# Four side-by-side products in the local attention output, and other transfer prices in the planner

## The chip, the cores and the metric

The kernel runs on one core of one Trainium2 chip, as one program. The metric is the device time of an execution in microseconds. A core has five engines that run side by side, each on its own list of instructions in fixed order: TensorE (PE), which multiplies matrices and writes the results into eight banks of PSUM; VectorE (DVE), ScalarE (ACT) and GpSimd (POOL), which work on elements; and SyncE (SP), which here issues nearly all transfers. The transfers run on DMA engines and land in SBUF or in device memory.

## The reference

Attention for 4 batches of 8 heads, 576 tokens of 64 features, is the sum of two parts; two expert layers follow on all 2304 tokens (512 features, 2048 hidden).

```python
q_d, k_d, v_d = (x.reshape(B, H, S // 4, 4, D).mean(axis=3) for x in (q, k, v))
out_up = np.repeat(sm_attn(q_d, k_d, v_d), 4, axis=2)          # pooled attention
mask = np.abs(pos[:, None] - pos[None, :]) < 4                 # local attention
scores = np.where(mask, scale * (q @ k.T), -1e9)
attn = exp(scores - max) ; attn = attn / (sum + 1e-9)
x = out_up + attn @ v                                          # per head
x = x.transpose(0, 2, 1, 3).reshape(B * S, H * D)
h = x @ w_in  ; x = (h * sigmoid(h)) @ w_out                   # layer 1
h = x @ w_in2 ; y = elu(h) @ w_out2                            # layer 2
```

## The kernel before

**Stages.** Attention works on 16 pairs of heads (four a batch). Layer 1's first half of the hidden features is computed beside it, in units of one block of 256 tokens and 128 hidden features: `first` (L983) multiplies the split input by the split weights, `second` (L1031) multiplies the activated result by the second weights. When these units are done, passes over pairs of token blocks follow (`paired`; first products on L1333, second ones on L1421 and L1423), for the rest of layer 1 and for layer 2. Numbers are carried as a high and a low part, so each product is three.

**One pair of heads** (`attend`). q and k rows are loaded (`load_rows`, L554), v for the pooled part (`load_v`, L558) and rows of v in ten overlapping windows of 64 (`load_windows`, L564 and L568). PE transposes q and k (L601), makes the local scores (`scores`, L712), the pooled scores (L765), and later transposes both softmax results (L818, L839). `out_d` (L857) gives the pooled output. `out_l` (L884) gives the local output, in two jobs of one half of the tokens (288) each: five windows by two heads, ten products with 64 rows and some 57 columns. Head j reads partitions 64j to 64j+63 and writes the same partitions of one PSUM bank, so the ten products alternate between two quarters of TensorE's array. `join` (L894, DVE) adds pooled and local output and writes x (`x32`). A product in 32-bit floats shows as two records in the trace.

The local scores use all four quarters: the windows alternate between column halves, the heads between row halves.

**The order of the work** is written out by a planner when the program is built. Each piece of work is a `Job` with an engine, an assumed duration, predecessors, buffers that it takes (`Hold`) and a due time. `pick` takes the job that can start first by the planner's clocks, among equals the one due first, and emits its instructions; each engine then runs its list in that order, whatever the real times are. For transfers the planner keeps one clock, `clock_of["dma"]`: a transfer begins after it, moves it on by the job's `dma` price, and lands a fixed time later; none is issued more than `BACKLOG` = 3 us ahead of it. Before the change the prices are 1.44 us for the rows of q or k of a pair, 1.6 for the window rows, 1.1 for v, 1.75 for a weight block of 512 KB, and 3.6 for the store of a batch's x.

```python
if self.dma is not None:
    clock_of["dma"] = max(clock_of["dma"], t + DMA_WAIT) + self.dma
    self.end = clock_of["dma"] + DMA_LAND
```

While `filling` is on (until layer 1's first unit is emitted) gaps that the planner sees on PE are filled with products of zeros (L328). `split_x` (L931 on ACT, L935 on GpSimd) splits x, `prepare` (L383 to L398, then L960 and L964) decodes and splits the weights. `keep_x` (L1070) stores a batch's x for the later passes; its job waits for all joins of that batch.

Of the kernel before, what the change touches and what calls it, by code (L numbers as in the profile page):

```python
# [15 lines left out]
ALU = mybir.AluOpType  # L16
# [6 lines left out]
def attention_moe_moe2_kernel(ctx, tc, q, k, v, wi1, wo1, wi2, wo2, out):  # L23
    nc = tc.nc
    B, H, S, D = q.shape
    NT, DM = out.shape
    DFF = wi1.shape[1]
    P = 128
    FAC = 4
    SD = S // FAC  # L30
    HS = SD // 2
# [10 lines left out]
    FP = NF // NPASS  # L42
# [131 lines left out]

    class Job:

        def __init__(self, eng, dur, fn, preds=(), gate=None, due=1e9, port=False, lat=0.1, other=None, takes=(), uses=(), dma=None, mode=None):
# [12 lines left out]
            self.sooner(due)  # L190
# [45 lines left out]
        def emit(self):  # L236
            t = self.start()
            assert t is not None
            cand.remove(self)
            for h in self.takes:  # L240
                h.take()
            if self.eng == "P":
                if filling[0]:
                    fill(t)
                mode_of[0] = self.mode
                now[0] = t + self.dur
            self.fn()
            clock_of[self.eng] = t + self.dur
            if self.port:
                clock_of["port"] = t + self.dur  # L250
            self.end = t + self.dur + self.lat
            if self.dma is not None:
                clock_of["dma"] = max(clock_of["dma"], t + DMA_WAIT) + self.dma
                self.end = clock_of["dma"] + DMA_LAND
# [110 lines left out]
    def decode_jobs(i, out, preds, takes=(), temp=None):  # L365
# [8 lines left out]
        if i < 2 * FP:  # L374
            held = [Hold(WS)]
            wst[i] = held[0]
            landed[i] = Job("S", 0.55, lambda: load_w(i), [], takes=held, dma=1.75)
        else:
            landed[i] = Job("S", 0.55, lambda: load_w(i), [decoded[i - WS_N]] if i >= 2 * FP + WS_N else [decoded[n] for n in range(2 * FP)], dma=1.75)

        def first():
            st = pairs_of(wst[i])
# [80 lines left out]
    def pool_matrix():  # L463
# [10 lines left out]
                )  # L474
        nc.vector.tensor_copy(m[WIN:P], m[:WIN])

    def pool_rows(w):

        return min(w0[1], w0[w + 1] - w0[w]) if w < NW - 1 else WIN
# [49 lines left out]
    def attend(i, due):  # L529
# [2 lines left out]
        h0 = 2 * pr  # L532
        early = b == 0
        packed = b < PACKED
        by_pe = b < PE_POOLED
# [35 lines left out]
        lq = Job("S", 1.1, lambda: load_rows(hq, q, nc.sync), [], takes=[hq], dma=cost)  # L571
        if early and pr < 2:
            lk = Job("A", 1.2, lambda: load_rows(hk, k, nc.scalar), [], takes=[hk], dma=cost)
        else:
            lk = Job("S", 1.1, lambda: load_rows(hk, k, nc.sync), [], takes=[hk], dma=cost)
        lw = Job("S", 2.2, load_windows, [], takes=[hw], dma=1.6)


        def tT():
# [2 lines left out]
        def row(which, c):  # L582
            return (hq, hk)[which].tile[:, c * 2 * D:(c + 1) * 2 * D]
# [6 lines left out]
        for n_, cells in enumerate(([(0, c) for c in range(NTB - 1)], [(1, c) for c in range(NTB - 1)], [(0, NTB - 1), (1, NTB - 1)])):  # L590
            bank = Hold(banks, "a")

            def flip(cells=cells, bank=bank):
                for n, (which, c) in enumerate(cells):
                    if packed:
                        for j in range(2):
                            nc.tensor.transpose(
                                bank.tile[j * D:(j + 1) * D, n * TB:(n + 1) * TB], row_of(which, j, c)[:TB], ident[:TB, :TB]
                            )
                    else:  # L600
                        nc.tensor.transpose(bank.tile[:, n * TB:(n + 1) * TB], row(which, c)[:TB], ident[:TB, :TB])  # L601

            used = {0: [hq], 1: [hk], 2: [hq, hk]}[n_]
            pj = Job(
                "P", (0.1 if packed else 0.085) * len(cells), flip, [lq] if n_ == 0 else [lk] if n_ == 1 else [lq, lk], lat=0.2,
                takes=[bank] + ([hqk] if n_ == 0 else []), uses=used, mode="t",
            )
            pj.after(prior)
            prior = [pj]
# [28 lines left out]
                    o += n  # L638


        red = Job(
            "V", 1.35, lambda: nc.vector.reduce_sum(hqkD.tile, hqk.tile.rearrange("p (m r) -> p m r", r=FAC), axis=AX.X),
            copies, takes=[hqkD], uses=[hqk],
        )
# [55 lines left out]
        for part, (s0, s1, halves_, outs) in enumerate(parts):  # L700
# [173 lines left out]
            for t in outs:  # L874
                bank = Hold(banks, "a")

                def out_l(t=t, bank=bank):
                    vw = hw.tile.rearrange("p (n d) -> p n d", d=D)
                    for w in range(t * NW // 2, (t + 1) * NW // 2):
# [11 lines left out]
                def join(t=t, bank=bank):  # L891
                    g0 = b * S + t * HALF
                    u0 = t * HALF // FAC
                    nc.vector.tensor_tensor(  # L894
                        x32[:, pr, g0:g0 + HALF].rearrange("p (m r) -> p m r", r=FAC),
                        bank.tile[:, :HALF].rearrange("p (m r) -> p m r", r=FAC),
                        haD.tile[:, u0:u0 + HALF // FAC].rearrange("p (m o) -> p m o", o=1).to_broadcast([P, HALF // FAC, FAC]),
                        op=ALU.add,
                    )

                pj = Job("P", 0.54, out_l, [lw] + [flips[g] for g in sorted(flips) if t == 1 or g == 0], lat=0.2, takes=[bank], uses=[hw, haT], mode="s")
                end_ = due[t] if isinstance(due, tuple) else due + 0.5 * t
                final.append(Job("V", 0.47, join, [pj, ups] + (sum(first_users.values(), []) if b == 1 else second_users if b else []), due=end_, uses=[bank, haD]))
                x_written[pr, 2 * b + t] = final[-1]
                if early:
                    first_users[pr].append(final[-1])
        batch_end.setdefault(b, []).extend(final)
        return final

# [535 lines left out]
    with tc.manual_schedule():  # L1445
# [52 lines left out]
            landed[i].due = W_AT  # L1498
        filler(WARM)
        constants()  # L1500
        pool_matrix()
        hpool.take()

        run(g1_jobs[0, 0])
        filling[0] = False
        run([j for b_ in range(B) for j in batch_end[b_]] + [kept_x[b_] for b_ in range(B)] + [x for p_ in w_split.values() for x in p_])
        PREFER.clear()
# [71 lines left out]
```

## Time and profile before

| | us |
|---|---|
| median of three runs | 909.17 |
| lowest | 908.99 |
| profiled execution | 908.4 |
| its span, first to last instruction | 906.7 |
| PE busy in the span | 886.6 |
| DVE busy | 640.9 |
| ACT busy | 535.1 |
| GpSimd busy | 258.7 |

One of the three runs took 2409.44 us; the median is not moved by it. The span is shorter than the execution by what lies around the first and last instruction. Attention ends at about 253 us of the span, layer 1's units at about 347 us. A row of the order of time reads: start, duration, engine, line, operation, what it writes and reads, shapes, the number of instructions merged, and in brackets the engine's idle time before it and what ended it.

### The profile page before, as it was taken

The numbers are of one execution on the slowest core, as the hardware profiler recorded it, in microseconds if no ns is written. First come the engines' busy times: TensorE is split into PE (matmuls) and PEld (weight loads), VectorE is DVE, ScalarE is ACT, GpSimd is POOL, SyncE is SP. The second block draws the span as 40 slices with busy tenths as digits, with TensorE's granted clock in tenths as the row PEclk, the third lists the DMA queues.
The fourth block names the chain that finished last, engine by engine and source line by source line (L and its number), as shares of the span: only waits on it lengthen the run. The fifth ranks groups of instructions, "written<-read, shape, count | busy, mean of one in ns | idle before, by whom it ended". The sixth has DMA issues, their size and how long they took to land.

```text
span 906.7 us, 17602 instructions
## 1 busy us (share of the span) xinstructions
PE 886.6 (98%) x6828; PEld 829.5 (91%) x6828; DVE 640.9 (71%) x1174; ACT 535.1 (59%) x1214; POOL 258.7 (29%) x280
## 2 busy tenths in 40 slices
PE   8979999999999999999999999999999999999998
PEld 5768899999999999999999999899898898998986
DVE  6888874556449847968948988669669889383562
ACT  4776474565447647637448568378388585471650
POOL 4687487666400101400105213001032023010000
PEclk9989899999999999999999999999999999999999
DMA  9796535353075121446153051340430530220301
GB/s 156 194 214 162 148 85 151 89 152 93 1 239 168 43 82 59 164 140 203 41 187 105 36 165 57 105 157 18 155 101 1 198 128 35 87 88 36 105 1 69
DMA packets 105730, 100.09 MB, mean 110 GB/s; under 512 B 62320, under 2 KB 88944, under 8 KB 105648
## 3 DMA queue, kind: packets, MB, share of 16 engines
q1 hardware_dynamic: 103280, 98.39, 36.8%
q8 instruction: 53, 0.87, 0.4%
q10 hardware_dynamic: 2368, 0.59, 0.4%
q14 instruction: 29, 0.24, 0.1%
HBM read 75.37 MB, written 23.59 MB: 109 GB/s over the span
## 4 chain that ended last, share of the span: by engine, by line
PE 57%; DVE 1%; issue 0%
PE b L1333 26%; PE b L1423 21%; PE b L1421 10%; DVE raw L398 0%; DVE part L1386 0%; DVE wl L1127 0%; DVE hgx L1231 0%; DVE raw L394 0%; DVE hg L1231 0%; DVE raw L391 0%
## 5 line engine op out<-in xcount | busy, mean ns | idle before, releaser
L1031 PE MATMUL b<-gh,wh 128*128 128x256 f32 x288 | 84.9, 295 | 0.0
L1031 PE MATMUL b<-gh,wl 128*128 128x256 f32 x288 | 82.4, 286 | 0.0
L1031 PE MATMUL b<-gl,wh 128*128 128x256 f32 x288 | 82.3, 286 | 0.0
L983 PE MATMUL b<-xh,wh 128*128 128x256 f32 x288 | 76.4, 294 | 0.2 <-DVE x L635 0.2
L1423 PE MATMUL b<-wl,grw 128*128 128x512 f32 x192 | 74.8, 389 | 0.0
L1423 PE MATMUL b<-wh,glk 128*128 128x512 f32 x192 | 74.8, 389 | 0.0
L1423 PE MATMUL b<-wh,ghk 128*128 128x512 f32 x192 | 74.7, 389 | 0.0
L1423 PE MATMUL b<-wh,grw 128*128 128x512 f32 x192 | 74.7, 389 | 0.0
L1333 PE MATMUL b<-xhr,wSA 128*128 128x384 f32 x288 | 74.5, 334 | 0.0
L983 PE MATMUL b<-xl,wh 128*128 128x256 f32 x288 | 73.8, 285 | 0.0
L983 PEld LDWEIGHTS b<-xh,wh 128*128 128x128 f32 x288 | 55.7, 193 | 2.1 <-issue 1.4
L1031 PEld LDWEIGHTS b<-gh,wh 128*128 128x128 f32 x288 | 55.9, 194 | 1.8 <-issue 1.2
L1031 PEld LDWEIGHTS b<-gl,wh 128*128 128x128 f32 x288 | 56.1, 195 | 0.0
L1031 PEld LDWEIGHTS b<-gh,wl 128*128 128x128 f32 x288 | 56.1, 195 | 0.0
L983 PEld LDWEIGHTS b<-xl,wh 128*128 128x128 f32 x288 | 55.7, 193 | 0.2
L1127 DVE TENSOR_TENSOR xlr<-xraw,xhr 128x768 fp32r<-128x768 f32 x46 | 44.4, 970 | 15.0 <-ACT xhr L1124 15.0
L1011 ACT ACTIVATE t<-b 128x256 f32<-128x256 f32 x72 | 27.5, 383 | 43.6 <-PE b L983 41.1
L1386 DVE SCALAR_TENSOR_TENSOR part<-b,part 128x384 f32<-128x384 f32 (+1 forms) x42 | 24.6, 612 | 40.1 <-PE b L1423 27.1
L1345 ACT COPY hg<-b 128x384 f32<-128x384 f32 x54 | 25.9, 480 | 45.7 <-PE b L1333 45.1
L1333 PEld LDWEIGHTS b<-xhr,wSA 128*128 128x128 f32 x288 | 52.1, 188 | 0.0
L983 PE MATMUL b<-xh,wl 128*128 128x256 f32 x288 | 50.7, 285 | 0.0
L1012 DVE SCALAR_TENSOR_TENSOR t<-t,b 128x256 f32<-128x256 f32 x72 | 29.9, 416 | 29.4 <-ACT t L1011 29.3
(289 smaller groups left out, 2803.4 us busy)
## 6 DMA issues: line engine op xcount, KB each, us to landing
ws<-in_moe_w_in_dram SPq DMA_DIRECT2D x32, 512.0 KB
ws<-in_moe_w_out_dram SPq DMA_DIRECT2D x32, 512.0 KB
xraw<-x SPq DMA_DIRECT2D x24, 384.0 KB
xd<-x SPq DMA_DIRECT2D x4, 1152.0 KB
yp<-yo SPq DMA_DIRECT2D x9, 512.0 KB
x<-part SPq DMA_DIRECT2D x6, 768.0 KB
yp<-yo SPq DMA_DIRECT2D x6, 768.0 KB
part<-yp SPq DMA_DIRECT2D x6, 768.0 KB
```

The costliest lines, as they stand in the source:

```text
L983: nc.tensor.matmul(ph.tile[:, :NB0], w[a][:, c, :], x_slot(n, c, b_), start=start and m == 0, stop=stop and m == len(products) - 1,)
L1011: th = Job("A", ACT_[NB0], lambda: nc.scalar.activation(tt(), h(), AF.Tanh, scale=0.5), [p2], takes=[t], uses=[ph])
L1012: st = Job("V", VEC_[NB0] + 0.02, lambda: nc.vector.scalar_tensor_tensor(tt(), tt(), 1.0, h(), op0=ALU.add, op1=ALU.mult), [th], uses=[ph])
L1031: nc.tensor.matmul(y[d // 2].tile[:, o:o + NB0], w[m // 2][:, sl], gg(m % 2), start=f == 0 and m == 0 and d % 2 == 0, stop=fin and m == 2, ...
L1127: other=("V", VEC_[width], lambda: nc.vector.tensor_tensor(lo(), src, hi().bitcast(F32), ALU.subtract)),
L1333: nc.tensor.matmul(acc_, a[:, cs], b[:, c, :], start=fresh and c == 0 and m == 0, stop=c == 1 and m == 2, skip_group_check=True,)
L1345: snap[after, j] = [Job("A", ACT_[NB], lambda dst=dst, acc_=acc_: nc.scalar.copy(dst, acc_), [], gate, due=soon)]
L1386: nc.vector.scalar_tensor_tensor(dst, src, sc, dst, op0=ALU.mult, op1=ALU.add)
L1421: nc.tensor.matmul(y[d][:, :NB], wm[:, sl], gm, start=first, stop=last_)
L1423: nc.tensor.matmul(y[d], gm[:, sl], wm, start=first, stop=last_)
```

## The change

For batches 2 and 3 (`QUAD_FROM = 2`) the two `out_l` jobs of a pair become one. It takes two banks, one for each half of the tokens, and walks through both halves in turn; in half 1 the heads write swapped column halves. So four successive products go to four different quarters. The adds of half 1 read swapped partitions and become two of 64 partitions each. Half 0 keeps its single add.

The planner's prices for transfers rise: rows of q and k to 1.6, window rows to 1.9, v to 1.5, weight blocks to 2.2 us. The store of batch 0's x waits for batch 1's joins instead of batch 0's (`X_AFTER = 1`). The other new names are set so that they change nothing (`POOL_QK = 0`, `FILL_TO = (0, 0)`, the `SAFE` values 0).

```diff
+    D_ROWS, D_LOCAL, D_V, D_W, S_ROWS, S_LOCAL, X_AFTER = 1.6, 1.9, 1.5, 2.2, 1.1, 2.2, 1
+    POOL_QK = 0
+    QUAD_FROM = 2
+    FILL_TO, SAFE_R, SAFE_W = (0, 0), 0.0, 0.0
-            landed[i] = Job("S", 0.55, lambda: load_w(i), [], takes=held, dma=1.75)
+            landed[i] = Job("S", 0.55, lambda: load_w(i), [], takes=held, dma=D_W, safe=SAFE_W)
-        cost = 1.05 if packed else 1.44
+        cost = 1.05 if packed else D_ROWS
-        lw = Job("S", 2.2, load_windows, [], takes=[hw], dma=1.6)
+        lw = Job("S", S_LOCAL, load_windows, [], takes=[hw], dma=D_LOCAL)
-            lv = Job("S", 1.1, load_v, [], takes=[hv], dma=1.1)
+            lv = Job("S", S_ROWS, load_v, [], takes=[hv], dma=D_V)
...
+            banko = [Hold(banks, "a") for _ in range(2)]
+
+            def out_l(banko=banko):
+                vw = hw.tile.rearrange("p (n d) -> p n d", d=D)
+                for i_ in range(NW // 2):
+                    for t in range(2):
+                        w = i_ + t * NW // 2
                         n = a0[w + 1] - a0[w]
                         c0 = (w % 2) * WIN + a0[w] - q0[w]
                         o = a0[w] - t * HALF
                         for j in range(2):
+                            p_ = (j + t) % 2 * D
                             nc.tensor.matmul(
-                                bank.tile[j * D:(j + 1) * D, o:o + n],
+                                banko[t].tile[p_:p_ + D, o:o + n],
...
+            pj = follow(Job("P", 0.75, out_l, [lw] + [flips[g] for g in sorted(flips)], lat=0.2, takes=banko, uses=[hw, haT], mode="s"), "pso")
+            for t, p0, p1 in ((0, 0, P), (1, 0, D), (1, D, P)):
...
+                    i0 = (p0 + t * D) % P
                     nc.vector.tensor_tensor(
-                        x32[:, pr, g0:g0 + HALF].rearrange("p (m r) -> p m r", r=FAC),
-                        bank.tile[:, :HALF].rearrange("p (m r) -> p m r", r=FAC),
+                        x32[p0:p1, pr, g0:g0 + HALF].rearrange("p (m r) -> p m r", r=FAC),
+                        bank.tile[i0:i0 + p1 - p0, :HALF].rearrange("p (m r) -> p m r", r=FAC),
...
-        kept_x[b] = Job("S", 0.6, go, batch_end[b], due=due, dma=3.6)
+        kept_x[b] = Job("S", 0.6, go, batch_end[max(b, X_AFTER)], due=due, dma=3.6)
```

## Rows read from the trace of the kernel before

**Rows 1.** The page, part 1: busy time, share, instructions of each engine.

```profile
PE 886.6 (98%) x6828; PEld 829.5 (91%) x6828; DVE 640.9 (71%) x1174; ACT 535.1 (59%) x1214; POOL 258.7 (29%) x280
```

**Rows 2.** Windows: length, busy PE, PEld, DVE, ACT, POOL; clock, DMA, GB/s.

```profile
120.00:253.00 133.00, 132.62 (x1715) 125.83 (x1714) 72.12 (x158) 71.95 (x228) 85.55 (x107) 1.00 0.35 94
253.00:347.00 94.00, 94.00 (x773) 94.00 (x772) 62.13 (x134) 54.06 (x122) 5.47 (x6) 1.00 0.40 128
...
386.00:906.00 520.00, 516.42 (x2710) 482.14 (x2710) 373.88 (x639) 306.29 (x603) 79.44 (x64) 1.00 0.29 97
```

**Rows 3.** Windows before 120 us; the last three are half-clock stretches.

```profile
54.00:62.00 8.00, 2.70 (x19) 2.35 (x19) 6.87 (x15) 5.32 (x15) 6.99 (x9) 0.81 1.21 237
...
84.00:90.00 6.00, 4.88 (x57) 4.06 (x58) 4.58 (x8) 3.31 (x8) 4.07 (x6) 0.69 0.02 4
...
59.02:65.84 6.82, 5.34 (x29) 5.34 (x30) 6.67 (x13) 4.34 (x13) 5.90 (x8) 0.50 1.14 231
...
86.33:93.15 6.82, 6.82 (x65) 5.99 (x64) 4.78 (x9) 3.58 (x9) 3.12 (x4) 0.50 0.12 27
...
106.81:110.21 3.40, 3.40 (x20) 3.06 (x20) 3.02 (x5) 0.63 (x3) 0.73 (x1) 0.50 0.05 11
```

**Rows 4.** Order of time of PE: its waits, and what ended them.

```profile
56.95 0.60 PE L601 MATMUL b<-ident,spare 96*128 96x96 f32 x5 [2.73 <-DMA spare<-in_q_dram]
...
60.50 1.03 PE L601 MATMUL b<-ident,nat 96*128 96x96 f32 x5 [2.57 <-DMA nat<-in_k_dram]
...
85.12 0.49 PE L839 MATMUL b<-ident,ring 72*72 72x72 f32 x4 [1.30 <-DVE ring L723]
...
106.22 0.52 PE L818 MATMUL b<-ident,ring 128*128 128x128 f32 x3 [1.75 <-DVE qk L630]
...
385.95 0.44 PE L1421 MATMUL b<-grw,wl 128*128 128x384 f32 x1 [1.33 <-DVE wl L1127]
```

**Rows 5.** Order of time of PE: local output L884, scores L712, successors.

```profile
230.42 0.79 PE L884 MATMUL b<-ring,vw 64*64 64x60 f32 x20
231.14 0.49 PE L839 MATMUL b<-ident,ring 72*72 72x72 f32 x4
...
249.77 1.38 PE L884 MATMUL b<-ring,vw 64*64 64x60 f32 x40
251.08 0.71 PE L857 MATMUL b<-ring,vd 72*64 72x144 f32 x8
...
73.18 0.81 PE L712 MATMUL b<-x 64*64 64x64 f32 x40
73.93 0.39 PE L983 MATMUL b<-xh,wh 128*128 128x256 f32 x1
```

**Rows 6.** Windows of one line: L884 in 141 to 251 us, L712.

```profile
sum 110.00, PE 11.51 PEld 10.18; mean PE 5.75 PEld 5.09
...
141.00:251.00 110.00, 5.85 (x280) 4.89 (x280) 1.00 0.34 89
```

**Rows 7.** Order of time of SP's queue: loads, and the stores of x.

```profile
49.42 0.91 SPq L554 DMA_DIRECT2D spare<-in_q_dram  x2
...
52.47 2.65 SPq L554 DMA_DIRECT2D nat<-in_k_dram  x2
...
72.25 0.58 SPq L1070 DMA_DIRECT2D xd<-x  x1
...
90.33 0.65 SPq L564 DMA_DIRECT2D vw<-in_v_dram  x1
...
136.45 0.56 SPq L1070 DMA_DIRECT2D xd<-x  x1
```

**Rows 8.** Order of time of POOL: splits done before the load waits end.

```profile
55.36 0.73 POOL L935 TENSOR_TENSOR xl<-x,xh 128x256 fp32r<-128x256 f32 x1
...
56.62 2.51 POOL L964 TENSOR_TENSOR wl<-wf,wh 128x512 fp32r<-128x512 f32 x2 [0.53 <-ACT wh L960]
```

**Rows 9.** Line L894, the add into x: ns min/median/max, first, last.

```profile
L894 DVE TENSOR_TENSOR x<-b,ring x28: 423/456/459, 26.2 to 252.6; 128x288 f32<-128x288 f32 x28
```

More of the change, by code (lines that the diff above doesn't have):

```diff
@@ L175, in attention_moe_moe2_kernel, with __init__ @@
     class Job:
-        def __init__(self, eng, dur, fn, preds=(), gate=None, due=1e9, port=False, lat=0.1, other=None, takes=(), uses=(), dma=None, mode=None):
+        def __init__(self, eng, dur, fn, preds=(), gate=None, due=1e9, port=False, lat=0.1, other=None, takes=(), uses=(), dma=None, mode=None, safe=0.0):
+            self.safe = safe
             self.eng, self.dur, self.fn, self.gate = eng, dur, fn, gate
@@ L253, in emit @@
                 clock_of["dma"] = max(clock_of["dma"], t + DMA_WAIT) + self.dma
-                self.end = clock_of["dma"] + DMA_LAND
+                self.end = clock_of["dma"] + DMA_LAND + self.safe
             for h in self.uses:
@@ L376, in decode_jobs @@
             wst[i] = held[0]
-            landed[i] = Job("S", 0.55, lambda: load_w(i), [], takes=held, dma=1.75)
+            landed[i] = Job("S", 0.55, lambda: load_w(i), [], takes=held, dma=D_W, safe=SAFE_W)
         else:
-            landed[i] = Job("S", 0.55, lambda: load_w(i), [decoded[i - WS_N]] if i >= 2 * FP + WS_N else [decoded[n] for n in range(2 * FP)], dma=1.75)
+            landed[i] = Job("S", 0.55, lambda: load_w(i), [decoded[i - WS_N]] if i >= 2 * FP + WS_N else [decoded[n] for n in range(2 * FP)], dma=D_W, safe=SAFE_W)
         def first():
@@ L475, in pool_matrix, with poolers, pool_matrices @@
         nc.vector.tensor_copy(m[WIN:P], m[:WIN])
+    def poolers():
+        n = len(POOLED_BY) * HS
+        return natv[:, n:n + 2 * (TB // FAC)].rearrange("p (n m) -> p n m", n=2)
+    def pool_matrices():
+        m = poolers()
+        nc.gpsimd.memset(m[:TB, 0], PSCALE)
+        nc.gpsimd.memset(m[:TB, 1], 1.0)
+        for sign, base_ in ((1, 0), (-1, FAC - 1)):
+            nc.gpsimd.affine_select(
+                out=m[:TB], in_=m[:TB], compare_op=ALU.is_ge, fill=0.0, base=base_,
+                pattern=[[0, 2], [-sign * FAC, TB // FAC]], channel_multiplier=sign,
+            )
     def pool_rows(w):
@@ L601, in flip @@
                         nc.tensor.transpose(bank.tile[:, n * TB:(n + 1) * TB], row(which, c)[:TB], ident[:TB, :TB])
+                if by_rows and len(cells) == 2:
+                    for which in range(2):
+                        for c in range(NTB):
+                            o = 2 * TB + which * SD + c * (TB // FAC)
+                            nc.tensor.matmul(
+                                bank.tile[:, o:o + TB // FAC], row(which, c)[:TB], poolers()[:TB, which, :], start=True, stop=True,
+                            )
             used = {0: [hq], 1: [hk], 2: [hq, hk]}[n_]
             pj = Job(
-                "P", (0.1 if packed else 0.085) * len(cells), flip, [lq] if n_ == 0 else [lk] if n_ == 1 else [lq, lk], lat=0.2,
-                takes=[bank] + ([hqk] if n_ == 0 else []), uses=used, mode="t",
+                "P", 0.085 * len(cells) + (1.1 if by_rows and n_ == 2 else 0.0), flip, [lq] if n_ == 0 else [lk] if n_ == 1 else [lq, lk], lat=0.2,
+                takes=[bank] + ([hqk] if n_ == 0 else []), uses=used + ([hpool] if by_rows and n_ == 2 else []), mode="t",
             )
@@ L638, in attend @@
                     o += n
-        red = Job(
+        n = 2 * SD
+        red = alike(
+            0.19 + 0.0008 * n, lambda bank=bank: nc.scalar.copy(hqkD.tile, bank.tile[:, 2 * TB:2 * TB + 2 * SD]),
+            0.15 + 0.00106 * n, lambda bank=bank: nc.vector.tensor_copy(hqkD.tile, bank.tile[:, 2 * TB:2 * TB + 2 * SD]),
+            [pj], takes=[hqkD], uses=[bank],
+        ) if by_rows else Job(
             "V", 1.35, lambda: nc.vector.reduce_sum(hqkD.tile, hqk.tile.rearrange("p (m r) -> p m r", r=FAC), axis=AX.X),
@@ L873, in attend, with out_l, join @@
                 second_users.extend([psl, red])
[L874 to L879, printed above, removed]
+            if b < QUAD_FROM:
+                for t in outs:
+                    bank = Hold(banks, "a")
+                    def out_l(t=t, bank=bank):
+                        vw = hw.tile.rearrange("p (n d) -> p n d", d=D)
+                        for w in range(t * NW // 2, (t + 1) * NW // 2):
+                            n = a0[w + 1] - a0[w]
+                            c0 = (w % 2) * WIN + a0[w] - q0[w]
+                            o = a0[w] - t * HALF
+                            for j in range(2):
+                                nc.tensor.matmul(
+                                    bank.tile[j * D:(j + 1) * D, o:o + n],
+                                    vw[j * WIN:(j + 1) * WIN, w, :],
+                                    aT()[j * WIN:(j + 1) * WIN, w // 2, c0:c0 + n],
+                                    start=True, stop=True,
+                                )
+                    def join(t=t, bank=bank):
+                        g0 = b * S + t * HALF
+                        u0 = t * HALF // FAC
+                        nc.vector.tensor_tensor(
+                            x32[:, pr, g0:g0 + HALF].rearrange("p (m r) -> p m r", r=FAC),
+                            bank.tile[:, :HALF].rearrange("p (m r) -> p m r", r=FAC),
+                            haD.tile[:, u0:u0 + HALF // FAC].rearrange("p (m o) -> p m o", o=1).to_broadcast([P, HALF // FAC, FAC]),
+                            op=ALU.add,
+                        )
+                    pj = Job("P", 0.54, out_l, [lw] + [flips[g] for g in sorted(flips) if t == 1 or g == 0], lat=0.2, takes=[bank], uses=[hw, haT], mode="s")
+                    end_ = due[t] if isinstance(due, tuple) else due + 0.5 * t
+                    final.append(Job("V", 0.47, join, [pj, ups] + (sum(first_users.values(), []) if b == 1 else second_users if b else []), due=end_, uses=[bank, haD]))
+                    x_written[pr, 2 * b + t] = final[-1]
+                    if early:
+                        first_users[pr].append(final[-1])
+                continue
@@ L889, in out_l, with join @@
                             )
-                def join(t=t, bank=bank):
+            pj = follow(Job("P", 0.75, out_l, [lw] + [flips[g] for g in sorted(flips)], lat=0.2, takes=banko, uses=[hw, haT], mode="s"), "pso")
+            for t, p0, p1 in ((0, 0, P), (1, 0, D), (1, D, P)):
+                bank = banko[t]
+                def join(t=t, bank=bank, p0=p0, p1=p1):
                     g0 = b * S + t * HALF
                     u0 = t * HALF // FAC
+                    i0 = (p0 + t * D) % P
                     nc.vector.tensor_tensor(
-                        x32[:, pr, g0:g0 + HALF].rearrange("p (m r) -> p m r", r=FAC),
-                        bank.tile[:, :HALF].rearrange("p (m r) -> p m r", r=FAC),
-                        haD.tile[:, u0:u0 + HALF // FAC].rearrange("p (m o) -> p m o", o=1).to_broadcast([P, HALF // FAC, FAC]),
+                        x32[p0:p1, pr, g0:g0 + HALF].rearrange("p (m r) -> p m r", r=FAC),
+                        bank.tile[i0:i0 + p1 - p0, :HALF].rearrange("p (m r) -> p m r", r=FAC),
+                        haD.tile[p0:p1, u0:u0 + HALF // FAC].rearrange("p (m o) -> p m o", o=1).to_broadcast([p1 - p0, HALF // FAC, FAC]),
                         op=ALU.add,
                     )
-                pj = Job("P", 0.54, out_l, [lw] + [flips[g] for g in sorted(flips) if t == 1 or g == 0], lat=0.2, takes=[bank], uses=[hw, haT], mode="s")
                 end_ = due[t] if isinstance(due, tuple) else due + 0.5 * t
-                final.append(Job("V", 0.47, join, [pj, ups] + (sum(first_users.values(), []) if b == 1 else second_users if b else []), due=end_, uses=[bank, haD]))
-                x_written[pr, 2 * b + t] = final[-1]
+                job = Job("V", 0.47, join, [pj, ups] + (sum(first_users.values(), []) if b == 1 else second_users if b else []), due=end_, uses=[bank, haD])
+                if p0:
+                    job.after([x_written[pr, 2 * b + t]])
+                final.append(job)
+                x_written[pr, 2 * b + t] = job
                 if early:
-                    first_users[pr].append(final[-1])
+                    first_users[pr].append(job)
         batch_end.setdefault(b, []).extend(final)
@@ L1500, in attention_moe_moe2_kernel @@
         constants()
+        if POOL_QK:
+            pool_matrices()
         pool_matrix()
@@ L1504, in attention_moe_moe2_kernel @@
         run(g1_jobs[0, 0])
+        run(g1_jobs[FILL_TO])
         filling[0] = False
```

9 lines of the change are left out of this document (5 added, 4 removed).

## The prediction

> **What bounds the kernel now.** I read the page's busy line first: TensorE (PE) is busy 886.6 of 906.7 us, the next engine, DVE, 640.9 [rows 1]. So time can only come from less PE work, from PE's idle stretches, or from a faster clock. The page averages over unlike stages, so the second view is the windows by stage [rows 2]. From 386 us on PE runs dense products to the end, and from 120 to 347 us it is busy 226.6 of 227 us at full clock: there a microsecond of PE work that is taken away is a microsecond off the end, as long as other work is ready behind it. It is: attention ends at about 253 us, and 94 us of layer 1's products, all PE, still stand behind it. Between 347 and 386 us PE stands idle once, 1.33 us, for the split of a second-product weight on DVE [rows 4].
>
> The third view is PE's order of time with what ended its waits [rows 4]. Before 120 us four waits matter: 2.73 and 2.57 us for a load of q and one of k (until 56.95 and 60.50), 1.30 for DVE's masking (until 85.12), 1.75 for a DVE copy (until 106.22); 8.35 us together. The windows of the granted clock [rows 3] show the second loss: 17.04 us at 0.50, that is 1.2 of 2.4 GHz, in three stretches from 59.02, 86.33 and 106.81 us, each beginning just after or within one of those waits. PE has 15.56 us of busy time there, which at full clock would take about half: some 8.5 us at most are lost by half of the 17.04. Waits and clock together are a pool of 8.35 + 8.5 = 16.9 us that a better order could at most recover.
>
> **The change, part by part.** *Four products side by side (batches 2 and 3, eight pairs of heads).* Nothing is removed from the count: each pair still has 20 products, 40 records. Today ten products of one half of the tokens (20 records) take 0.72 us from their start to the next instruction's, and both halves in one go take 1.31 us (249.77 to 251.08) [rows 5]. They use two quarters of the array in turn: rows 0-63 with columns 0-63, rows 64-127 with columns 64-127. The nearest row for four quarters is the local scores (L712): products of the same height, 64 columns instead of 57, that change through all four; their 40 records take 0.75 us (73.18 to 73.93) [rows 5]. So a pair saves 1.31 - 0.75 = 0.56 us if its halves stand together today and 1.44 - 0.75 = 0.69 if apart: 4.5 to 5.5 us for eight. The busy windows give 11.51 us for the eight pairs and 5.85 for seven runs of the scores [rows 6]: 1.44 - 0.84 = 0.60 a pair, 4.8 for eight. Three of the eight overlap with the scores already, so I take 4.7. Below that lies nothing saved (a rival), above it 5.5.
>
> Here a page speaks against the change. In the trace the local output's two row halves already write one PSUM bank and take 0.72 us for ten products, where the scores, whose row halves write different banks, take 0.75 for twenty [rows 5]. The Trainium skill, page TensorEngine Tiling (Array Packing), section Restrictions and Gotchas, says that different row tiles cannot access the same PSUM bank at once. The new order puts one half of the tokens, both row halves, in one bank, so by that rule the pair could stay near 1.31 us and the sum below would lose its first term.
>
> *The third add.* Half 1's columns land swapped, so its add into x becomes two of 64 partitions. One add over 288 columns takes a median of 0.456 us [rows 9]; half the partitions should not change that, so 8 x 0.456 = 3.6 us more DVE. Between 120 and 253 us DVE is busy 72 of 133 us and PE is the bound [rows 2], so I cost it at nothing; without that cover it is 3.6 us. The product now takes two PSUM banks at once and waits for both transposed groups instead of the first alone. The first half's product is late by at most the time of the second copy and PE has layer-1 products to place in it, so I cost that at nothing; uncovered it would be one run of 20 records a pair, 8 x 0.72 = 5.8.
>
> *The longer transfers in the planner.* They move no byte; they change the hand-written order. Rows go from 1.44 to 1.6 us, window rows 1.6 to 1.9, v 1.1 to 1.5, a weight block 1.75 to 2.2. The trace says how good the new ones are: from 54 to 62 us the queues move 237 GB/s [rows 3], so a block of 512 KB needs 524288 / 237000 = 2.2 us, and a 288 KB load 1.24. At the two load waits: the queue takes a weight block, v, a weight block and q of a pair (issued 49.42), then a weight block and k (52.47) [rows 7]. The planner priced the first four at 6.04 us and now at 7.5, and the two after them at 3.19, now 3.8: it will put q's transposes 1.46 us and k's 2.07 us later, and other products ahead. Was there other work? GpSimd finished a split of x at 56.09 and two weight splits by 59.13 us [rows 8], while PE stood until 56.95 and 60.50. So 0.86 and 1.37 us of the waits had ready work behind them, 2.2 us; the rest was want of data. I take the smaller number, 2.1. The bounds are wider: nothing, and the pool's 16.9 us, if the reordering also happens to part the clusters before 85 and 106 us. On the other side, the planner now sees batch 0's eight row loads and four window loads 8 x 0.16 + 4 x 0.3 = 2.5 us later and will fill that with warm-up products; I cost that at nothing because the data waits at 54 to 62 us absorb a later start, 2.5 us if they don't. The weight price also holds for the later passes, where PE has no idle but 1.33 us [rows 4]; I leave that as it is.
>
> *Batch 0's x stored behind batch 1.* The 1152 KB store is issued at 72.25 us now [rows 7]. The last PE wait for a load ends at 60.50 [rows 4], before it, and at 84 to 90 us the DMA engines stand nearly still (4 GB/s) [rows 3], because the next load, at 90.33, waits for a buffer that PE frees. So taking the store away there frees nothing: 0. It goes to about 132 to 137 us, next to batch 1's (136.45) [rows 7]. On SP it is one issue of 0.58 us; the price of the company is a rival.
>
> **Sum.** 4.7 + 2.1 = 6.8 us off the profiled execution's 908.4 us (span 906.7): 901.6. The median of the runs is 909.17, 0.8 above that, so 902.4.
>
> **The rivals.** *The front stage is largely cured.* For it: the two load waits are just the kind that true prices avoid, and two half-clock stretches follow waits of under 2 us, so a little can free much. Against: at 54 to 62 us DVE (6.87 of 8) and GpSimd (6.99) are nearly full [rows 3], so data, not order, is short. If two thirds of the 16.9 us come back: 4.7 + 11.3 = 16 off, 893.
>
> *Slower: the two stores together stop the loads behind them.* At 237 GB/s the extra 1152 KB is 1179648 / 237000 = 5.0 us in the one queue through which the loads of the next pairs come. For it: PE's order is fixed, a transpose whose rows are late stops all behind it, as at 56.95. Against: from 120 to 253 us the DMA share is 0.35 and PE idles 0.38 us in all [rows 2]. If a wait of 5.0 us appears, with a half-clock stretch like the shorter of the three after it (3.4 at half, 1.7) and no gain in front, the sum is +6.7 - 4.7 = 2.0 slower, 911. It decides once PE waits more than 4.7 us there.
>
> *The four don't run side by side.* If it is the bank, or something else that the local output has and the scores have not, that sets 0.72 us for ten products, 40 records stay at 1.31 us and only 2.1 come off, 907. For it: no row shows four quarters with both row halves on one bank. Against: in the scores, too, each bank takes two products at once, from its two column halves.
>
> **How the numbers follow.** Forecast 0.62 (own range 898 to 907, from the terms' ends 4.5 to 5.5 and 0 to 4), cured front 0.13, stores or a worse order 0.18, no side by side 0.07. The predicted time is the forecast's, 902.4. The range 890 to 912 leaves out the best of the cured case (a full pool would be 909.2 - 21.6 = 888) and what is worse than 911. Two per cent, about what a measurement of this kernel tells from no change, is 18.2 us: faster than 891.0 needs 13.5 of the 16.9 us besides the quads, under half of the second case, 0.07; slower than 927.4 needs two new stalls with their clock, 0.02; within, 0.91.
>
> **What would show it.** In the changed kernel's trace a run of 40 local-output records should take 0.75 us in batches 2 and 3 and 1.3 to 1.45 in batch 1; three adds a pair; PE still without idle from 120 to 347 us, the end of attention about 5 to 7 us earlier. The load waits near 57 and 60 us should shrink to about 3 us together. I am wrong if the 40 records take 1.3 us, if a wait for a load shows after 130 us, if the half-clock total differs from 17 us by more than 7, or if the wait before 386 us grows by what PE has gained.

## The result and the profile after

The changed kernel takes 897.24 us, median of four runs (896.86 to 898.19), against 909.08 for the kernel before, measured beside it: a ratio of 0.9888 with an interval of 0.985 to 0.9926, 11.8 us faster. The forecast was 902.4 us, a gain of 6.8; the time lies in the stated range of 890 to 912 us, just below the 898 to 907 that the forecast named as its own, and the gain is larger than forecast.

The windows of the changed kernel by stage (length, busy us of PE, PEld, DVE, ACT, POOL, clock, DMA share, GB/s):

```profile
0.00:44.00 44.00, 41.86 (x680) 30.27 (x684) 33.70 (x74) 25.08 (x82) 23.28 (x41) 1.00 0.83 163
44.00:62.00 18.00, 13.52 (x159) 11.52 (x155) 15.13 (x31) 14.74 (x37) 17.28 (x21) 0.88 0.99 232
62.00:120.00 58.00, 56.59 (x663) 52.28 (x661) 51.30 (x89) 41.68 (x113) 45.29 (x43) 0.98 0.55 141
120.00:245.00 125.00, 123.10 (x1671) 116.24 (x1671) 70.23 (x157) 68.35 (x215) 77.38 (x98) 1.00 0.39 108
...
245.00:337.00 92.00, 92.00 (x756) 92.00 (x755) 61.21 (x130) 52.94 (x119) 5.68 (x6) 1.00 0.40 128
```

And the three stages of the kernel before that [rows 2] and [rows 3] leave out:

```profile
0.00:44.00 44.00, 39.59 (x665) 29.79 (x666) 33.51 (x73) 25.42 (x83) 23.63 (x41) 1.00 0.88 176
44.00:62.00 18.00, 11.60 (x153) 9.72 (x153) 15.74 (x30) 14.06 (x37) 15.19 (x20) 0.92 0.90 202
62.00:120.00 58.00, 54.70 (x605) 50.62 (x605) 47.58 (x85) 34.92 (x89) 36.98 (x39) 0.88 0.62 154
```

Read the idle part of PE: up to 120 us it was 4.4 + 6.4 + 3.3 = 14.1 us and is 2.1 + 4.5 + 1.4 = 8.0. From 62 to 120 us the clock rose from 0.88 to 0.98. But from 120 us to the end of attention PE stands 1.9 us, where it stood 0.4 [rows 2].

The order of time of PE in the changed kernel: its largest waits, then local output and scores of the same kind as in [rows 5].

```profile
57.75 1.03 PE L621 MATMUL b<-ident,spare 96*128 96x96 f32 x5 [3.95 <-DMA spare<-in_q_dram]
...
101.02 0.49 PE L871 MATMUL b<-ident,ring 72*72 72x72 f32 x4 [0.45 <-DVE qk L657]
...
142.80 0.71 PE L797 MATMUL b<-qkD 64*72 64x144 f32 x8 [1.04 <-DVE qkD L674]
...
376.48 0.44 PE L1499 MATMUL b<-grw,wl 128*128 128x384 f32 x1 [0.17 <-DVE wl L1205]
...
64.71 1.38 PE L917 MATMUL b<-ring,vw 64*64 64x60 f32 x40
66.02 0.71 PE L889 MATMUL b<-ring,vd 72*64 72x144 f32 x8
...
136.35 0.81 PE L955 MATMUL b<-ring,vw 64*64 64x60 f32 x40
137.09 0.63 PE L621 MATMUL b<-ident,spare 96*128 96x96 f32 x5
```

Of the four waits before 120 us [rows 4] one is left, 3.95 us for a load of q. The wait for weights before 386 us, 1.33 us, is 0.17. Forty records of local output take 1.31 us in batch 1 (64.71 to 66.02) and 0.74 in batch 2 (136.35 to 137.09). One half-clock stretch is left before 120 us, where [rows 3] show three:

```profile
57.69:64.52 6.83, 6.68 (x33) 6.04 (x33) 5.37 (x13) 4.62 (x15) 5.28 (x6) 0.50 0.84 205
```

New is a wait of DVE. The order of time of DVE, and below it SP's two stores of x, now close together:

```profile
138.61 1.41 DVE L970 TENSOR_TENSOR x<-b,ring 64x288 f32<-64x288 f32 x3 [4.02 <-DMA xd<-x]
```

```profile
126.63 1.28 SPq L1148 DMA_DIRECT2D xd<-x  x1
...
130.75 0.56 SPq L1148 DMA_DIRECT2D xd<-x  x1
```

**How runs are compared below.** Repeated executions of one kernel differ by several microseconds, and the difference goes with the clock: 13 runs of the kernel before lie between 903.63 us (mean granted clock 0.995) and 910.03 (0.988). So each run's span is also multiplied by its mean clock. That product is about what the run would take at full clock; the rest of the span is at most what the clock cost, since a wait inside a slow stretch need not be shorter at full clock. The kernel before, run again beside each group of experiments, has medians of 908.03, 907.69 and 908.04 us (13, 15 and 19 runs), so medians of different groups are set side by side; the changed kernel has its four runs alone. Means over the runs of each kernel:

| kernel | median us | span x clock | clock's share |
|---|---|---|---|
| before (13 runs, beside e1 to e4) | 908.03 | 896.7 | 8.9 |
| changed | 897.24 | 891.8 | 3.8 |
| e1 prices and store, no quads | 901.74 | 894.8 | 5.4 |
| e2 quads alone | 902.29 | 892.8 | 7.2 |
| e3 changed, store back | 900.49 | 893.1 | 5.9 |
| e4 changed, two quarters | 901.82 | 895.6 | 4.3 |
| e5 changed, old weight price | 905.75 | 895.8 | 7.8 |
| e6 changed, old attention prices | 899.23 | 890.5 | 7.6 |
| e7 changed, prices halfway | 904.26 | 894.6 | 7.9 |
| e9 changed, store by pair | 895.64 | 889.9 | 4.3 |
| e10 changed, fourth add | 899.50 | 894.1 | 3.6 |
| e11 changed, products ahead of the wrong pair | 897.84 | 893.2 | 2.9 |
| e12 e9 with the wait filled | 894.42 | 891.5 | 0.9 |
| e13 before, new weight price alone | 904.32 | 895.0 | 7.5 |

Of the 10.1 us between the mean spans of the first two rows 5.0 are work and waits, 5.1 are clock.

The front of the kernel also varies by itself. e4 and e10 below have the changed kernel's order up to 130 us, and yet its row of 101.02 us stands over 1 us later in their profiled runs, by PE's order of time in e4, then in e10:

```profile
102.32 0.49 PE L871 MATMUL b<-ident,ring 72*72 72x72 f32 x4 [0.45 <-DVE qk L657]
```

```profile
102.06 0.49 PE L871 MATMUL b<-ident,ring 72*72 72x72 f32 x4 [0.45 <-DVE qk L657]
```

So a difference of about 1 us between two kernels is read here only where the trace shows where it arises.

### The profile page after: what moved, and what is told of

It is laid out like the page before. It is cut to its first block, busy times and chain, and to the rows that moved or that the text cites. A ratio compares the mean times of both kernels' runs of the same rounds, so it can differ in the third digit from the quotient of the medians.

```text
span 895.1 us, 17620 instructions
## 1 busy us (share of the span) xinstructions
PE 880.7 (98%) x6836; PEld 821.5 (92%) x6836; DVE 642.1 (72%) x1173; ACT 536.1 (60%) x1220; POOL 263.0 (29%) x282
## 4 chain that ended last, share of the span: by engine, by line
PE 57%; DVE 2%; issue 0%
PE b L1411 26%; PE b L1501 22%; PE b L1499 10%; DVE raw L403 1%; DVE raw L399 0%; DVE wl L1205 0%; DVE part L1464 0%; DVE b L1419 0%; DVE glk L1205 0%; DVE raw L396 0%; DVE hgx L1309 0%; DVE ghk L1205 0%; DVE hg L1309 0%
## 5 line engine op out<-in xcount | busy, mean ns | idle before, releaser
L768 POOL TENSOR_TENSOR ring<-ring,small 128x640 f32<-128x640 f32 x30 | 38.8, 1294 | 45.2 <-DVE small L763 22.5
```

The costliest lines, as they stand in the source:

```text
L768: eng.tensor_tensor(E3(s0, s1), E3(s0, s1), col3(h, s0, s1).to_broadcast([P, 2 * (s1 - s0), WIN]), op)
```

## The experiments

**Is it the four quarters? (e4)**

```diff
-                            p_ = (j + t) % 2 * D
+                            p_ = j * D
...
-                    i0 = (p0 + t * D) % P
+                    i0 = p0
```

> The changed kernel with every instruction in its place, but half 1's products go to the same two quarters of the array as half 0's (column halves not swapped). Theory: a run of 40 records takes 1.31 us again instead of 0.74, the end is 8 x 0.57 = 4.5 us later, about 901.7 us. Rival, the gain lies in making one job of two, not in the four quarters: within 1 us of the changed kernel.

Measured: 901.82 us, 4.6 more than the changed kernel, 3.8 by span times clock. Every engine's list is the same. The order of time of PE in e4:

```profile
137.68 1.38 PE L955 MATMUL b<-ring,vw 64*64 64x60 f32 x40
138.99 0.63 PE L621 MATMUL b<-ident,spare 96*128 96x96 f32 x5
```

1.31 us again instead of 0.74, for eight pairs 8 x 0.57 = 4.6 us. So the four quarters are worth 3.8 to 4.6 us at the end, all or most of the PE work that they save. One job in place of two gives nothing beyond the 1.31 us that two halves took before where they stood together [rows 5].

**The parts apart (e1, e2, e3).**

```diff
-    QUAD_FROM = 2
+    QUAD_FROM = 4
```

> The changed kernel with the local output of all batches in two jobs as before, and two adds a pair; the new transfer prices and the later store stay. Theory: the quads are worth their PE time, 0.56 to 0.70 us a pair, 4.5 to 5.5 us in all, and the front stage's gain comes from the prices alone: the time is about 902 us, and the waits before 62 us and the single half-clock stretch are those of the changed kernel. Rival, all of the 11.8 us hangs on one lucky order: the order differs anywhere and the time is anywhere between 897 and 910, with other waits before 120 us too.

```diff
-    D_ROWS, D_LOCAL, D_V, D_W, S_ROWS, S_LOCAL, X_AFTER = 1.6, 1.9, 1.5, 2.2, 1.1, 2.2, 1
+    D_ROWS, D_LOCAL, D_V, D_W, S_ROWS, S_LOCAL, X_AFTER = 1.44, 1.6, 1.1, 1.75, 1.1, 2.2, 0
```

> The kernel before with only the quads for batches 2 and 3 (old prices, store of batch 0's x behind batch 0). Theory: up to 120 us it is the kernel before, with its four waits (8.35 us) and 17 us at half clock, and it gains only 4.5 to 5.5 us: about 904 us. Rival, the quads also change the order before 120 us: under 901 us, or no gain.

```diff
-    D_ROWS, D_LOCAL, D_V, D_W, S_ROWS, S_LOCAL, X_AFTER = 1.6, 1.9, 1.5, 2.2, 1.1, 2.2, 1
+    D_ROWS, D_LOCAL, D_V, D_W, S_ROWS, S_LOCAL, X_AFTER = 1.6, 1.9, 1.5, 2.2, 1.1, 2.2, 0
```

> The changed kernel with the store of batch 0's x behind batch 0 again. In the changed kernel the two stores stand close together (126.6 and 130.8 us), DVE waits 4.02 us for a store before the first add of batch 2 and PE then stands 1.04 us. Theory: moving the store gave nothing and cost about 1 us, so this runs in 896 to 897 us, without that DVE wait. Rival, the later store freed the queues for loads before 100 us and is part of the gain: 900 us or more, with more idle PE before 120 us.

Measured: 901.74, 902.29 and 900.49 us. Prices and store alone gain 6.3 us, quads alone 5.7; together 10.8 against the same base; by span times clock it is about 2, 4 and 5 us. e1's clock share is 5.4 us, where I expected the changed kernel's 3.8: in its profiled run, the slowest of the six, the clock stays at half for 17.07 us in one piece:

```profile
56.92:73.99 17.07, 14.35 (x101) 12.95 (x100) 11.99 (x22) 9.71 (x26) 12.03 (x14) 0.50 0.69 164
```

e2 gains a little more than the 4.5 to 5.5 us that I expected of it, and its front is not quite that of the kernel before: it keeps the kernel before's wait at 83.51 us and trades the one at 106 for another, by the order of time of PE:

```profile
83.51 0.49 PE L871 MATMUL b<-ident,ring 72*72 72x72 f32 x4 [1.29 <-DVE ring L755]
...
99.01 0.39 PE L1061 MATMUL b<-xh,wh 128*128 128x256 f32 x1 [3.10 <-DVE x L662]
```

e3 contradicts what I expected of it: with the store back it is 3.3 us slower, 1.3 of it work and waits, 2.0 clock. It has no DVE wait for a store, but it has another order from about 90 us on and a wait of its own, for a DVE result:

```profile
98.90 0.63 PE L621 MATMUL b<-ident,nat 96*128 96x96 f32 x5 [1.32 <-DVE t L1090]
```

So the late store is part of the gain, but e3 can't tell the transfer from the order that it changes. e9 can, for what the late store costs.

**What does the wait for the store cost? (e9)**

```diff
-            nc.sync.dma_start(xd[b], x32[:, :, b * S:(b + 1) * S])
+            for c_ in range(KC):
+                nc.sync.dma_start(xd[b][:, c_, :], x32[:, c_, b * S:(b + 1) * S])
```

> The changed kernel with each store of a batch's x in four transfers, one for each pair of heads, in the same place of SP's list. Theory: DVE's wait of 4.02 us for a store before batch 2's first add comes from the store's transfer covering, from its first to its last address, the columns that the add writes; split by pair it does not, the wait and the 1.04 us of PE behind it go, and the time falls by about 1 us, to 896. Rival, the wait has another cause (the add follows the store in any case): DVE still waits 3 us or more for a store and the time is unchanged.

Measured: 895.64 us, 1.6 less than the changed kernel, the same order but for the stores. The same place in DVE's order of time, in e9:

```profile
137.47 1.41 DVE L970 TENSOR_TENSOR x<-b,ring 64x288 f32<-64x288 f32 x3 [2.77 <-PE b L955]
```

The add now waits for its own product, not for a store, and PE's wait of 1.04 us at 142.80 is gone. The add begins 1.14 us earlier: about that much of the 4.02 us was the store's alone, in the rest of it the product wasn't ready either. The add writes other columns than the store reads. In the trace of the changed kernel it waits for the semaphores (the counters by which one engine tells another that work is done) of both stores, in e9 for none of a store's. So the wait was put into the program when it was built, because one four-part transfer spans the addresses that the add writes.

**Which price? (e5, e6, e13, e7)**

```diff
-    D_ROWS, D_LOCAL, D_V, D_W, S_ROWS, S_LOCAL, X_AFTER = 1.6, 1.9, 1.5, 2.2, 1.1, 2.2, 1
+    D_ROWS, D_LOCAL, D_V, D_W, S_ROWS, S_LOCAL, X_AFTER = 1.6, 1.9, 1.5, 1.75, 1.1, 2.2, 1
```

> The changed kernel with the weight blocks at the old price of 1.75 us (rows, window rows and v at the new ones). Theory, truer prices avoid waits: part of the gain before 120 us goes, the waits near 57 and 60 us grow to about 5 us again, the time is 899 to 902 us. Rival, any other order would do as well, the gain over the kernel before is that its waits near 85 and 106 us and their half-clock stretches have no counterpart: within 2 us of the changed kernel.

```diff
-    D_ROWS, D_LOCAL, D_V, D_W, S_ROWS, S_LOCAL, X_AFTER = 1.6, 1.9, 1.5, 2.2, 1.1, 2.2, 1
+    D_ROWS, D_LOCAL, D_V, D_W, S_ROWS, S_LOCAL, X_AFTER = 1.44, 1.6, 1.1, 2.2, 1.1, 2.2, 1
```

> The changed kernel with the old prices for rows, window rows and v (1.44, 1.6, 1.1) and the new one for weight blocks. Theory, truer prices avoid waits: the transposes of q and k stand earlier again, the waits near 57 and 60 us are 4.5 to 5.5 us together, time 899 to 902 us. Rival, any other order: within 2 us of the changed kernel.

e13 is e6 with `X_AFTER = 0` and `QUAD_FROM = 4`.

> The kernel before with one number changed: weight blocks priced at 2.2 us instead of 1.75 (no quads, other prices old, store of batch 0's x behind batch 0). e5 lost nearly all of the gain with that price alone put back. Theory, the weight price carries most of what the prices give: about 902 to 904 us, half-clock loss and the wait near 385 us as in the changed kernel. Rival, no price carries it by itself, an order is good or bad as a whole: 906 us or more.

```diff
-    D_ROWS, D_LOCAL, D_V, D_W, S_ROWS, S_LOCAL, X_AFTER = 1.6, 1.9, 1.5, 2.2, 1.1, 2.2, 1
+    D_ROWS, D_LOCAL, D_V, D_W, S_ROWS, S_LOCAL, X_AFTER = 1.52, 1.75, 1.3, 1.975, 1.1, 2.2, 1
```

> The changed kernel with all four prices halfway between old and new (1.52, 1.75, 1.3, 1.975). Theory, truer prices give less waiting step by step: between e2's 902.3 and the changed kernel's 897.2, that is 899 to 901 us. Rival, the planner's order jumps with any number: outside of that, below 897 or above 903 us.

Measured: e5 905.75, e6 899.23, e13 904.32, e7 904.26 us. The weight price alone, put back, costs 8.5 us, more than either case that I had set down for e5 (899 to 902 us, or within 2 us of the changed kernel). Alone, put in, it gains 3.7; e13 misses the 902 to 904 us of its theory by 0.3, and its clock share is 7.5 us, not the changed kernel's 3.8. The three attention prices together are worth 2.0 by the median, which fits both cases of e6, and e6 is even ahead by span times clock (890.5): it loses more to the clock. But halfway prices are not half as good; at 904.3 they are outside what the theory of truer prices allowed, on the rival's side. e5's losses, from PE's order of time, stand before 120 us and near 382 us, and the second place is one that I had left as it is:

```profile
58.93 0.68 PE L850 MATMUL b<-ident,ring 128*128 128x128 f32 x3 [3.34 <-DVE x L927]
...
108.86 0.39 PE L1061 MATMUL b<-xh,wh 128*128 128x256 f32 x1 [1.63 <-DVE t L1090]
...
382.49 0.44 PE L1499 MATMUL b<-grw,wl 128*128 128x384 f32 x1 [2.81 <-DVE wl L1205]
```

The wait near 382 us is for the later passes' weights, whose loads have the weight price too. In the profiled runs it is 1.33 us before, 1.88 in e7, 2.81 in e5 and, in two pieces, 2.04 in e2, all with a lower price; with 2.2 us 0.2 or none in the changed kernel and the other runs but e3, where it is 1.33 again. And it can cost clock: e5's windows at half clock, the second right behind that wait, are

```profile
59.15:72.80 13.65, 12.50 (x91) 10.77 (x90) 7.76 (x17) 7.38 (x20) 8.02 (x11) 0.50 0.84 189
383.42:386.83 3.41, 3.41 (x13) 3.41 (x12) 2.03 (x6) 0.51 (x1) 0.00 (x0) 0.50 0.02 5
```

**Is the third add free? (e10)** Half 0's add is split in two as half 1's is.

```diff
+                    for a_, z_ in ([(p0, p1)] if t else [(0, D), (D, P)]):
+                        y0 = i0 + a_ - p0
...
```

> The changed kernel with half 0's add also split into two of 64 partitions, in its place: eight DVE instructions of about 0.456 us more, 3.6 us of DVE in all. Theory, DVE is covered by PE there: within 0.7 us of the changed kernel's 897.2. Rival, the adds lie on the path through the split of x: 2 to 4 us slower.

Measured: 899.50 us, 2.3 more, and 2.3 more by span times clock too. Apart from the eight adds every engine's list is the same. From 120 to 245 us PE is busy 121.16 us, 1.9 less than in the changed kernel. The window of that stage, then two of PE's waits:

```profile
120.00:245.00 125.00, 121.16 (x1655) 114.13 (x1656) 72.08 (x161) 67.81 (x214) 78.66 (x100) 1.00 0.40 108
```

```profile
173.21 0.39 PE L1063 MATMUL b<-xh,wh 128*128 128x256 f32 x1 [0.43 <-DVE x L972]
...
187.26 0.39 PE L1063 MATMUL b<-xh,wh 128*128 128x256 f32 x1 [0.43 <-DVE x L972]
```

In both rows, from the order of time of PE, it waits for a DVE result of line 972, the add. The orders of time of DVE and ACT at the first of them:

```profile
171.76 1.88 DVE L972 TENSOR_TENSOR x<-b,ring 64x288 f32<-64x288 f32 x4 [0.69 <-PE b L955]
```

```profile
173.19 0.41 ACT L1011 CAST xh<-x 128x256 fp32r<-128x256 f32 x1 [1.67 <-DVE x L972]
```

The split of x begins together with the product, so the product can't be reading that split, as the rival had it. The third of the four adds ends at 173.16, just before the product starts; what is left that the two share is a bank of PSUM, which the adds read and the product may then write. That is argued from the order, not tested. The stage's other larger waits of PE are for DVE results as well, and DVE's wait for a store is still in e10 (4.16 us); what a fourth add costs without that wait was not run. DVE is busy little more than half of that stage, and still 3.6 us more of it cost 2.3.

The third add, though, costs next to nothing. The same window in e9, without the wait for the store, and in e3, both with three adds a pair:

```profile
120.00:245.00 125.00, 124.44 (x1685) 117.65 (x1684) 70.86 (x158) 69.41 (x218) 77.64 (x98) 1.00 0.42 119
```

```profile
120.00:245.00 125.00, 125.00 (x1686) 117.50 (x1685) 69.93 (x156) 68.23 (x218) 79.03 (x99) 1.00 0.37 100
```

PE stands 0.56 us in e9 and not at all in e3, where the kernel before stands 0.38 [rows 2].

**Does the clock fall for that wait? (e11, e12)**

```diff
...
+                if first_:
+                    one_ = ident.bitcast(BF16)
+                    for _ in range(FILL_WAIT):
+                        nc.tensor.matmul(bank.tile[:, :2 * P], one_[:, :P], one_[:, :2 * P], start=True, stop=True)
                 for n, (which, c) in enumerate(cells):
...
```

> The changed kernel with 24 products of an unused constant (128 rows, 256 columns, bf16, about 2.6 us together) put in PE's list ahead of the transposes that wait 3.95 us for a load of q (57.75 us). They compute nothing that is used. Theory: the half-clock stretch of 6.83 us begins in that wait because PE stands idle, so with PE kept busy the clock stays at 1.0, and the time falls by up to 3.4 us, to 894 us, the load's own wait being no longer. Rival, the clock falls for the time of day or for the small products around it, not for that wait: still a half-clock stretch near 57 us, time 897 us or more.

I had counted the pairs wrongly: in e11 the 24 products stood at 50.13 us, ahead of transposes that waited for nothing, and pushed the rest later. It ran in 897.84 us, and doesn't put the question: PE still stands 2.25 us until 60.54, and 3.41 us at half clock follow from 61.21.

> The stores by pair of e9, and 32 products of an unused constant (about 3.5 us together) in PE's list right before the transposes that wait 4.47 us for a load of q at 58.25 us in e9 (in e11 the products stood before an earlier pair's transposes). They compute nothing that is used; all else is in e9's order. Theory: the clock falls there because PE stands idle, so with PE busy it stays at 1.0 and the time falls by up to 3.4 us from e9's 895.6, to 892 or 893. Rival, the clock falls for the small products around the wait, or whatever the engine does: still 3.4 or 6.8 us at half clock near 57 us and 895 us or more.

e12 has 32 products at the right place. Measured: 894.42 us, 1.2 less than e9. The windows from 54 to 66 us, e9 first, then e12:

```profile
54.00:66.00 12.00, 7.68 (x73) 7.00 (x73) 10.05 (x21) 9.34 (x26) 10.13 (x12) 0.72 0.93 230
```

```profile
54.00:66.00 12.00, 9.28 (x116) 8.38 (x114) 11.33 (x20) 8.91 (x23) 10.36 (x13) 1.00 1.04 228
```

The clock stays at 1.00 where e9 has 0.72, and the mean share that the clock costs falls from 4.3 to 0.9 us. So at this place the clock fell because PE stood still. Of the 3.4 us only 1.2 by the medians, 1.8 by the means, reach the end: the products themselves waited for a DVE result until 55.55 us and ended after the load had come, so that the transposes began at 59.04 us instead of 58.25, and PE then stands 1.48 us more for DVE, which is busy 11.33 of these 12 us:

```profile
55.55 3.65 PE L618 MATMUL b<-ident 128*128 128x256 bf16 x32 [1.24 <-DVE wf L404]
59.04 0.58 PE L626 MATMUL b<-ident,spare 96*128 96x96 f32 x5
...
61.44 0.36 PE L1066 MATMUL b<-xh,wh 128*128 128x256 f32 x1 [1.48 <-DVE wf L404]
```

e12 is the fastest of all, ratio 0.9856 to the kernel before (0.9825 to 0.9887), ahead of the changed kernel.

## Why the prediction was right, and where it was not

**Right: the quads.** 4.7 us were forecast and 4.6 measured by the medians, 3.8 by span times clock (e4). The local scores were the right row to read the duration from: 0.75 us forecast, 0.74 measured. The Trainium skill, page TensorEngine Tiling (Array Packing), section Restrictions and Gotchas, says that different row tiles cannot access the same PSUM bank at once. The trace shows no cost of it here: both row halves write one bank, in its two partition halves, and 40 records take 0.74 us with two banks in turn. The rival with no gain falls.

**Right, but with no margin: the third add at nothing.** With three adds a pair PE stands 0.56 us of 125 in e9 and not at all in e3, so neither the add nor the second bank, also put at nothing, shows a cost. The reason given, that DVE is busy 72 of 133 us, could not show that: at about the same share a fourth add costs 2.3 us (e10).

**Too small: the longer prices at 2.1 us.** This is the term of the sum that failed. It counted only the two load waits, and only the part of them for which work stood ready; the gain by clock, and the waits at 85 and 106 us, were left to the rival of a cured front. e1 measures the term together with the store: 6.3 us by the medians, and by the table 1.9 of work and waits and 3.5 of clock. So the clock that goes with the waits is what the term lacked. The load waits did shrink: 5.30 to 3.95 us, where I had said about 3. But the waits at 85 and 106 us went as well (0.45 us near 101 is the largest left there), with them the two half-clock stretches that followed, and in the changed kernel the clock's share fell from 8.9 to 3.8 us. That is half of the gain, and my own criterion said so: half clock was to stay within 7 us of 17 and it went to 6.83.

**Two slips of the sum.** The ends named for the terms, 4.5 to 5.5 and 0 to 4 us, give 900 to 905 us, not the 898 to 907 written. And the pool of 16.9 us counts some 0.7 us twice, since part of one wait lies inside the first half-clock stretch, where PE is busy 5.34 of 6.82 us [rows 3].

**Also missed: the later passes.** The weight price, which I left as it is there, most likely took 1.2 us off the wait before 386 us; e3, with the same price and 1.33 us of wait, says that the order has a part in it.

**The ledger.** It is drawn up from the two profiled runs, whose spans differ by 906.7 - 895.1 = 11.6 us. Quads, 8 x 0.57: 4.6 off. The wait before 386 us, 1.33 - 0.17: 1.2 off. Idle PE from 120 us to the end of attention, 1.9 - 0.4: 1.5 on, of which 1.04 behind the store. Clock, as half of PE's busy time in the half-clock stretches before 120 us, (15.56 - 6.68) / 2: 4.4 off. PE's idle time before 120 us went from 14.1 to 8.0, -6.1, but the planner also filled its longer gaps with more products of zeros, by the groups of PE's lines up to 60 us (busy us and mean ns behind the bar), the kernel before first:

```profile
L328 PE MATMUL b<-t 128*128 128x512 bf16 x36 | 10.9, 428 | 2.2 <-DVE t L1447 1.4 <-ACT ring L826 0.6 <-ACT ring L845 0.2
```

```profile
L333 PE MATMUL b<-t 128*128 128x512 bf16 x44 | 14.0, 447 | 1.7 <-DVE t L1525 1.4 <-ACT spare L858 0.3
```

So 3.1 us of the 6.1 are filled, not gained, and 3.0 off remain. Sum: 11.7 off, against 11.6. That it closes to a tenth is partly luck: it is one run of each kernel, and by the table's means the quads give 3.8.

**The store.** "0" was right of the transfer at 72 us by the DMA rows, yet the place mattered: e3 is 3.3 us slower with the store in front, most likely through the order that it changes. The slower rival had the right place, two stores together near 130 us, and the wrong victim: no load was late; an add waited 4.02 us, 1.14 of it for a store alone, and PE 1.04.

**What stays open.** Whether true prices or just another order made the front better. e5 and e13 speak for the weight price, e7 against any smooth rule; with five price settings this can't be settled. How much of the clock's share belongs to any one wait is open too, as the last section shows.

## What to carry to other kernels

Put small products so that successive ones use different quarters of the array, and read what that gives from a line that does so already. Where an order is planned from prices, count not only the waits that a price mends but the clock that each wait takes along, and expect the whole order to move. A busy share of one half does not tell whether one more instruction is free: here the third add was, and the fourth cost 2.3 us. And look at what a program waits for when a transfer has gaps between its parts: a write into a gap can be made to wait for it.

## What the runs showed of the hardware

A short wait of PE can cost more in clock than in time, and need not. In the kernel before the clock was at half for 6.82 us after a wait of 1.30 us among small transposes at 85 us [rows 3, 4]. In e2 the same wait, 1.29 us at 83.51, and one of 3.10 us at 99.01 cost no clock in the profiled run:

```profile
64.00:120.00 56.00, 51.60 (x633) 48.24 (x632) 49.93 (x88) 37.12 (x98) 39.11 (x39) 1.00 0.59 149
```

Nor did the 1.33 us among dense products before 386 us, in the kernel before:

```profile
380.00:400.00 20.00, 18.67 (x108) 18.35 (x107) 17.88 (x29) 6.09 (x12) 3.49 (x2) 1.00 0.23 79
```

In e5, 2.81 us at that place took 3.41 us at half clock with them. Even with one kernel the loss varies: the kernel before ran from 903.63 to 910.03 us as its mean clock went from 0.995 to 0.988, and e2's six runs have mean clocks from 0.989 to 0.996. With PE kept busy through most of the wait by products that serve nothing, the profile of e12 has no half-clock stretch between its first 7 and its last 2 us; its own waits of 1.24 and 1.48 us brought none.
